# Attention outputs with tokens on partitions, row sums from a column of ones, and zero stores in portions

## The chip, the cores and the metric

The kernel runs on one core of a Trainium2 chip. Its time is the time on the device in microseconds (us). The engines are TensorE (PE, with its weight loads as PEld), VectorE (DVE), ScalarE (ACT), GpSimd (POOL) and SyncE (SP), which here only issues DMAs. Three timed runs of the kernel before and one profiled execution are at hand.

## The reference

Three stages follow each other: attention with a local window and some global columns, a dense MLP with the mish activation, and a mixture of eight experts with one expert per token.

```python
# q, k, v: [2, 8, 768, 64]; n_global = 8, n_local = 96
scores = q @ k.T / 8 - slope[h] * dist
keep = (col < n_global) | ((0 <= row - col) & (row - col < n_local))
a = exp(scores - max) where keep;  a = a / (sum(a) + 1e-9)
x = (a @ v) as [1536 tokens, 512]
h = x @ w_in;  x = (h * tanh(softplus(h))) @ w_out      # d_ff = 2048
e = argmax(x @ w_gate);  out = p[e] * (relu(x @ w1[e]) @ w2[e])   # 8 experts, d_ff = 1024
```

## The kernel before, in words

The 1536 tokens are cut into twelve tiles `t` of 128. A tile sees at most 232 columns of scores: 96 older tokens and 8 global ones (the part `c = 0`), and its own 128 (`c = 1`). Attention works in half tiles `s` (four of the eight heads each, 24 in all), through these steps:

- `a_S` (L285) makes the scores of four heads in PSUM, with queries on partitions.
- `a_max` (L295, DVE) adds the bias and takes the row maximum, `a_exp` (L312, ACT) the exponential. Its `accum_out` also writes the sum of the row into `rcs`, by an extra accumulator read on ACT.
- `a_T` transposes the probabilities on PE, and `a_Tev` (L354, ACT) copies them to `PT`, first part 0 and then part 1.
- `a_V` (L364) multiplies with the values. The values are the weights (64 columns, one head), `PT` is streamed (128 columns), and the output has channels on partitions and tokens along the free dimension, two heads in the two halves of the partitions.
- Because tokens lie along the free dimension there, the reciprocal row sums must be turned as well: `a_recip` (L319, DVE) adds 1e-9, inverts and spreads them to 512 columns, `a_R` transposes them on PE in four pieces, `a_Rc` (L333, ACT) copies them out of PSUM.
- `a_xm` (L387, DVE) multiplies outputs and reciprocals, `a_xh` (L396, ACT) rounds to float32r and `a_xl` (L400, DVE) forms the rest. Two tiles make a block of x, which is also stored for later passes.

The MLP works in 48 units `u` (three passes over w_in/w_out, six blocks of x): `L1_mms` (24 matmuls into `hp`), a chain of eleven mish steps on ACT and DVE that ends in `gh` and `gl`, and two units later `L2_mms` (12 matmuls into `acc`). The first ten units are interleaved with attention, two half tiles per unit. The MLP weights come as 32 chunks (`next_raw`), each converted in three parts by `next_conv`: part 0 is three integer operations on DVE, part 1 a rounding on ACT, part 2 a subtraction on DVE.

At the start an order written out by hand holds for all engines but SyncE, up to half tile 4. PE is kept busy by `fill` (a float32 matmul of the identity) while the first loads are under way. The two integers come by DMA and are needed for the bias (`bias_part`), the bias for the first `a_max`. From half tile 5 on the framework's scheduler sets the order of each engine by priority and its own prices, and may move independent work (such as conversions) forward. All loads are issued from SyncE, in its order; the integers from ACT. `load_v` brings 136 rows for a batch's first tile and 232 for the others. PSUM is one pool of eight banks.

Before the experts begin, the rows of their buffers `xg` are filled with zeros by `prefill`, 24 stores of 112 rows. It is called after unit 16:

```python
        if u == 16:
            prefill()
```

Of the kernel before, what the change touches and what calls it, by code (L numbers as in the profile page):

```python
# [34 lines left out]
NWARM = 17  # L35
# [7 lines left out]
def moe_kernel(ctx, tc, q, k, v, n_global, n_local, w_in, w_out, w_gate, w1, w2, out, dbg=None):  # L43
# [17 lines left out]
    int_raw = const.tile([128, 2, 2], I32, name="int_raw")  # L61
    for i_, src_ in enumerate((n_local, n_global)):
        nc.scalar.dma_start(int_raw[:, i_, :], src_.bitcast(I32).unsqueeze(0).broadcast_to([128, 2]))
# [4 lines left out]
    def make_ints():  # L68
        f = const.tile([128, 2, 2], F32, name="int_f")
        nc.vector.tensor_copy(f, int_raw)  # L70
        neg = const.tile([128, 2], F32, name="int_n")
        nc.vector.tensor_single_scalar(neg, f[:, :, 0], 0.0, op=ALU.is_lt)
        nc.vector.tensor_add(neg, neg, f[:, :, 1])
        nc.vector.scalar_tensor_tensor(out=nlg, in0=neg, scalar=4294967296.0, in1=f[:, :, 0],
                                       op0=ALU.mult, op1=ALU.add)

# [159 lines left out]
    def load_v(t):  # L236
        b, i = divmod(t, TPB)
        s0 = i * 128
        vv = at.tile([128, 2, DM], F32, tag="vv", name="vv")

        def ld(r0, n, col, tok):
            nc.sync.dma_start(vv[r0:r0 + n, col], v[b * S + tok:b * S + tok + n, :])

        if i == 0:
            ld(0, 128, 1, 0)
            nc.gpsimd.memset(vv[0:KR, 0], 0.0)
            ld(0, NG, 0, 0)
        elif i % 2 == 0:
# [3 lines left out]
        else:  # L252
# [29 lines left out]
    rcs = {}  # L282
    rbs = {}
# [11 lines left out]
    def a_max(s, q_):  # L295
        t, pr = divmod(s, 2)
        _, w, d0, _ = geom(t)
        if q_ == 0:
            Ps[s] = at.tile([128, 4, WN], F32, tag="P", name="P")
            mxs[s] = sm.tile([128, 4], F32, tag="mx", name="mx")  # L300
            if pr == 0:
                rcs[t] = sm.tile([128, H], F32, tag="su", name="su")
# [9 lines left out]
    def a_exp(s, q_):  # L312
        t, pr = divmod(s, 2)
        w = geom(t)[1]
        h = 4 * pr + q_
        nc.scalar.activation(out=Ps[s][:, q_, 0:w], in_=Ps[s][:, q_, 0:w], func=AF.Exp,  # L316
                             bias=mxs[s][:, q_:q_ + 1], scale=-1.0, accum_out=rcs[t][:, h:h + 1])

    def a_recip(t):  # L319
        su = rcs.pop(t)  # L320
        nc.vector.tensor_scalar_add(su, su, 1e-9)
        nc.vector.reciprocal(su, su)
        sp_ = xe.tile([128, ROW], F32, tag="x2", name="sp_")[:, 0:DM]
        nc.vector.tensor_copy(sp_.rearrange("p (a b) -> p a b", b=64), su.unsqueeze(2).to_broadcast([128, H, 64]))
        rbs[t] = sp_

    def a_R(t):
        rb = ps.tile([128, 4, 128], F32, tag="b", name="rb")
        for p_ in range(4):
            nc.tensor.transpose(rb[:, p_, :], rbs[t][:, p_ * 128:p_ * 128 + 128], ident)  # L330
        rbs[t] = rb

    def a_Rc(t):  # L333
        rs = xe.tile([128, ROW], F32, tag="x2", name="rs")[:, 0:DM].rearrange("p (a b) -> p a b", a=4)
        nc.scalar.copy(rs, rbs[t])
        rbs[t] = rs
# [27 lines left out]
    def a_V(s):  # L364
# [4 lines left out]
        if pr == 0:  # L369
            av_ps[t] = ps.tile([128, 4, 128], F32, tag="b", name="av")  # L370
        av = av_ps[t]
        va = vv[0:nk, 0]
        vb = vv[:, 1]
        for i in range(2):
            for c in range(2):
                for j in range(2):
                    q_ = 2 * i + j
                    h = 4 * pr + q_
                    hs = slice(h * 64, h * 64 + 64)
                    lh = va[:, hs] if c == 0 else vb[:, hs]  # L380
                    rh = PT[0:nk, 0, q_, :] if c == 0 else PT[:, 1, q_, :]
                    nc.tensor.matmul(av[64 * j:64 * j + 64, 2 * pr + i, :], lhsT=lh, rhs=rh,
                                     start=(c == 0), stop=(c == 1))
# [3 lines left out]
    def a_xm(t):  # L387
# [4 lines left out]
        xm = rbs.pop(t)  # L392
        nc.vector.tensor_mul(xm, av_ps.pop(t), xm)
        return xm

    def a_xh(t, xm):  # L396
        blk, o = divmod(t, 2)
# [1043 lines left out]
```

## Time and profile before

| what | value |
|---|---|
| three timed runs | 600.24, 602.90, 603.83 us, median 602.90 |
| profiled execution, its time | 601.62 us |
| its span | 599.8 us |
| busy: PE, DVE, ACT, POOL | 575.7 (96%), 480.0 (80%), 378.7 (63%), 88.4 us (15%) |
| DMA | 109.97 MB in 54935 packets |

The span is the time from the first to the last instruction of the profiled execution; its own time is 1.8 us longer. Busy shares are averages over stages that differ: attention with the first ten units lies before 157 us, the rest of the MLP up to about 385 us, the experts after it. Matmuls are pipelined, so a busy PE isn't PE at its peak.

### The profile page before, as it was taken

Reading aid. Unit: us, or ns where it says so; the run is one execution under the profiler, and the core shown is the slowest. Engines: PE = TensorE matmul, PEld = TensorE weight load, DVE = VectorE, ACT = ScalarE, POOL = GpSimd, SP = SyncE. Lnnn points to the kernel's source line nnn. Section 1 sums busy time; section 2 is a strip of 40 time slices with the busy share of each in tenths; the row PEclk is TensorE's granted clock in tenths of the full one; section 3 lists DMA queues with packets and bytes.
Section 4 is the critical chain, followed back from the end, with each engine's and each line's share of the span. In section 5 each row is a group of like instructions: output and inputs, shape, how many; then the busy total and the mean of one; then the engine's idle time right before and its main releaser. Section 6 shows DMA issues by size and latency. Waiting matters only on the chain.

```text
span 599.8 us, 11918 instructions
## 1 busy us (share of the span) xinstructions
PE 575.7 (96%) x4288; PEld 518.5 (86%) x4288; DVE 480.0 (80%) x1151; ACT 378.7 (63%) x882; POOL 88.4 (15%) x157
## 2 busy tenths in 40 slices
PE   8988999999999999999999999989999999999994
PEld 7766777777889899898989889779999999999994
DVE  5999999999699899776867667655985678888942
ACT  3898788898676565656455555465664566776731
POOL 3211210000110010010210301121201212113111
PEclk9999999999999999999999999999999999999998
DMA  7976555756899856322221310367667284586200
GB/s 225 343 246 190 179 209 172 241 191 229 282 304 300 326 187 227 113 71 80 98 89 54 106 36 36 114 251 281 203 243 251 96 310 164 199 307 235 106 18 22
DMA packets 54935, 109.97 MB, mean 183 GB/s; under 512 B 5723, under 2 KB 12891, under 8 KB 54866
## 3 DMA queue, kind: packets, MB, share of 16 engines
q1 hardware_dynamic: 48882, 90.21, 45.0%
q0 software_dynamic: 5696, 18.89, 9.6%
q8 instruction: 36, 0.59, 0.4%
q14 instruction: 33, 0.27, 0.1%
q10 hardware_dynamic: 288, 0.00, 0.0%
HBM read 84.67 MB, written 25.10 MB: 183 GB/s over the span
## 4 chain that ended last, share of the span: by engine, by line
PE 66%; DVE 15%; ACT 11%; DMA 5%; issue 2%; SPq 0%; POOL 0%; DVEq 0%; ACTq 0%; POOLq 0%
PE hp L441 18%; PE acc L460 16%; PE bacc L724 6%; PE bhp L724 6%; ACT P L316 3%; PE bacc L725 3%; PE bhp L725 3%; DVE P L305 2%; ACT PT L362 2%; DVE bw L158 2%; PE bhp L727 1%; PE bacc L727 1%; PE bacc L729 1%; PE bacc L728 1%; PE bhp L728 1%
## 5 line engine op out<-in xcount | busy, mean ns | idle before, releaser
L460 PE MATMUL acc<-wpair,gh 128*128 128x512 f32 x384 | 123.8, 400 | 1.4 <-ACT gh L497 1.4
L441 PE MATMUL hp<-xh,wpair 128*128 128x256 f32 x768 | 121.0, 287 | 2.3 <-ACT xh L398 2.2
L441 PEld LDWEIGHTS hp<-xh,wpair 128*128 128x128 f32 x768 | 104.3, 188 | 9.8 <-ACT xh L398 4.2
L460 PEld LDWEIGHTS acc<-wpair,gh 128*128 128x128 f32 x384 | 68.1, 188 | 16.5 <-issue 1.9
L158 DVE TENSOR_TENSOR bw<-bst,bw 128x512 fp32r<-128x512 f32 x112 | 72.9, 685 | 9.7 <-ACT bw L157 8.9
L157 ACT CAST bw<-bst 128x512 fp32r<-128x512 f32 x112 | 64.5, 620 | 19.6 <-PE bhp L728 9.8
L460 PE MATMUL acc<-wpair,gl 128*128 128x512 f32 x192 | 75.4, 393 | 0.8 <-DVE gl L500 0.8
L468 ACT ACTIVATE e<-hp 128x512 f32<-128x512 f32 x48 | 28.7, 598 | 71.3 <-PE hp L441 71.3
L441 PE MATMUL hp<-xl,wpair 128*128 128x256 f32 x384 | 63.9, 284 | 0.3 <-DVE xl L404 0.3
L724 PE MATMUL bhp<-xc,bw 128*128 128x352 f32 (+4 forms) x192 | 59.3, 364 | 0.7 <-DVE t L759 0.6
L724 PE MATMUL bacc<-hc,bw 128*128 128x352 f32 (+4 forms) x192 | 59.2, 364 | 0.0
L316 ACT ACTIVATE P<-P,mx 128x232 f32<-128x232 f32 (+1 forms) x96 | 44.7, 470 | 15.1 <-DVE mx L305 15.0
L441 PEld LDWEIGHTS hp<-xl,wpair 128*128 128x128 f32 x384 | 52.8, 188 | 1.0 <-DVE xl L404 0.9
L725 PE MATMUL bhp<-xc,bw 128*128 128x176 f32 (+4 forms) x192 | 48.5, 253 | 0.0
L725 PE MATMUL bacc<-hc,bw 128*128 128x176 f32 (+4 forms) x192 | 48.3, 252 | 0.0
L478 DVE SCALAR_TENSOR_TENSOR n<-n,r 128x512 f32<-128x512 f32 x48 | 33.1, 689 | 16.7 <-ACT r L476 15.9
L460 PEld LDWEIGHTS acc<-wpair,gl 128*128 128x128 f32 x192 | 36.1, 188 | 8.8 <-DVE gl L500 1.3
L500 DVE SCALAR_TENSOR_TENSOR gl<-n,gh 128x512 fp32r<-128x512 f32 x48 | 33.0, 688 | 11.6 <-ACT gh L497 10.6
L497 ACT ACTIVATE gh<-n 128x512 fp32r<-128x512 f32 x48 | 30.1, 628 | 13.4 <-DVE n L493 13.2
L472 ACT ACTIVATE n<-e 128x512 f32<-128x512 f32 x48 | 30.3, 632 | 13.1 <-DVE e L470 13.0
L724 PEld LDWEIGHTS bhp<-xc,bw 128*128 128x128 f32 x192 | 36.1, 188 | 1.7 <-DVE t L759 0.8
L423 POOL DMA_DIRECT2D xl<-xs x12 | 6.9, 576 | 204.9 <-PE hp L441 137.1
(220 smaller groups left out, 1278.2 us busy)
## 6 DMA issues: line engine op xcount, KB each, us to landing
bst<-in_moe_w_dram SPq DMA_DIRECT2D x56, 512.0 KB
wst<-in_moe_w_in_dram SPq DMA_DIRECT2D x16, 512.0 KB
wst<-in_moe_w_out_dram SPq DMA_DIRECT2D x16, 512.0 KB
xl<-xs POOLq DMA_DIRECT2D x12, 512.0 KB, 4.0
xh<-xs POOLq DMA_DIRECT2D x12, 512.0 KB, 4.9
xpl<-xps SPq DMA_DIRECT2D x24, 256.0 KB
xg<-z SPq DMA_DIRECT2D x24, 224.9 KB
w0f<-in_moe_w_dram SPq DMA_DIRECT2D x8, 512.0 KB
```

The costliest lines, as they stand in the source:

```text
L157: nc.scalar.copy(hi, src)
L158: nc.vector.tensor_sub(lo, src, hi.bitcast(F32))
L316: nc.scalar.activation(out=Ps[s][:, q_, 0:w], in_=Ps[s][:, q_, 0:w], func=AF.Exp, bias=mxs[s][:, q_:q_ + 1], scale=-1.0, accum_out=rcs[t][ ...
L441: yield lambda f=f, kk=kk, wi=wi, xx=xx, cs=cs: nc.tensor.matmul(hp[:, f, :], lhsT=w[:, wi, kk, cs], rhs=xx[:, kk, :], start=(kk == 0 and ...
L460: yield lambda f=f, o=o, cs=cs, gi=gi, wi=wi, first=first, last=last: nc.tensor.matmul(accs[b][o], lhsT=gi[:, cs], rhs=w[:, wi, f, :], sta ...
L468: nc.scalar.activation(out=e, in_=hp, func=AF.Exp, scale=-1.0)
L472: nc.scalar.activation(out=n, in_=e, func=AF.Square)
L478: nc.vector.scalar_tensor_tensor(out=n, in0=n, scalar=0.25, in1=r, op0=ALU.add, op1=ALU.mult)
L497: nc.scalar.mul(gts[u][0], n, -(2.0 ** -80))
L500: nc.vector.scalar_tensor_tensor(out=gl, in0=n, scalar=-(2.0 ** -80), in1=gh.bitcast(F32), op0=ALU.mult, op1=ALU.subtract)
L724: nc.tensor.matmul(o[:, 0:2 * cap], lhsT=wh, rhs=xc, start=first, stop=False)
L725: nc.tensor.matmul(o[:, 0:cap], lhsT=wl, rhs=xh, start=False, stop=last)
```

## The change

The roles in `a_V` are exchanged. `PT` is now the weight (64 tokens at a time) and the values are streamed: 64 columns of a head and a 65th that holds ones. The output has tokens on partitions, and its 65th column is the sum of the row. So `a_exp` writes no sum, and `a_recip`, `a_R` and `a_Rc` fall away. A new step `a_n` per half tile adds 1e-9 to the four sums, inverts them and multiplies the four heads, out of PSUM. Then `a_X` transposes the tile's 512 channels in four pieces, and `a_xh` and `a_xl` read its result in PSUM. Part 1 is now multiplied before part 0.

The tile of values has 65 columns per head; the ones are set by GpSimd, and the load writes 64 columns of each head, with a gap. The integers are loaded to one partition, and a matmul with a matrix of ones spreads them. There are 6 warm-up calls in place of 17, 3 calls after the integers, and the 4 later ones are gone. The order at the start is written anew around these steps; the loop is left to the scheduler as before. `prefill` becomes a generator, and three of its stores are made after each of the units 14 to 21.

```diff
-NWARM = 17
+NWARM = 6
...
-    int_raw = const.tile([128, 2, 2], I32, name="int_raw")
+    int_raw = const.tile([1, 2, 2], I32, name="int_raw")
...
-        nc.scalar.dma_start(int_raw[:, i_, :], src_.bitcast(I32).unsqueeze(0).broadcast_to([128, 2]))
+        nc.scalar.dma_start(int_raw[:, i_, :], src_.bitcast(I32).unsqueeze(0))
...
-    def make_ints():
-        f = const.tile([128, 2, 2], F32, name="int_f")
+    def make_ints(z, one, warm):
+        f = const.tile([1, 2, 2], F32, name="int_f")
...
-        neg = const.tile([128, 2], F32, name="int_n")
+        neg = const.tile([1, 2], F32, name="int_n")
...
-        nc.vector.scalar_tensor_tensor(out=nlg, in0=neg, scalar=4294967296.0, in1=f[:, :, 0],
+        nc.vector.scalar_tensor_tensor(out=z[0:1, :], in0=neg, scalar=4294967296.0, in1=f[:, :, 0],
...
+        nc.tensor.matmul(warm[:, 0:2], lhsT=one, rhs=z, start=True, stop=True)
+        nc.vector.tensor_copy(nlg, warm[:, 0:2])
...
     def load_v(t):
...
-        vv = at.tile([128, 2, DM], F32, tag="vv", name="vv")
+        vv = at.tile([128, 2, H, D + 1], F32, tag="vv", name="vv")
...
         def ld(r0, n, col, tok):
-            nc.sync.dma_start(vv[r0:r0 + n, col], v[b * S + tok:b * S + tok + n, :])
+            nc.sync.dma_start(vv[r0:r0 + n, col, :, 0:D],
+                              v[b * S + tok:b * S + tok + n, :].rearrange("p (h d) -> p h d", d=D))
+        def one(r0, n, col):
+            nc.gpsimd.memset(vv[r0:r0 + n, col, :, D:D + 1], 1.0)
+        one(0, 128, 1)
...
+            one(0, NG, 0)
...
-        elif i % 2 == 0:
+        else:
+            one(0, NPRE, 0)
+        if i > 0 and i % 2 == 0:
...
-        else:
+        elif i > 0:
...
-    rcs = {}
-    rbs = {}
+    xns = {}
+    xps_ = {}
...
     def a_S(s):
...
-            if pr == 0:
-                rcs[t] = sm.tile([128, H], F32, tag="su", name="su")
...
     def a_exp(s, q_):
...
-        h = 4 * pr + q_
...
-                             bias=mxs[s][:, q_:q_ + 1], scale=-1.0, accum_out=rcs[t][:, h:h + 1])
-    def a_recip(t):
...
-    def a_R(t):
...
-    def a_Rc(t):
...
+                             bias=mxs[s][:, q_:q_ + 1], scale=-1.0)
...
-        if pr == 0:
-            av_ps[t] = ps.tile([128, 4, 128], F32, tag="b", name="av")
-        av = av_ps[t]
-        va = vv[0:nk, 0]
-        vb = vv[:, 1]
-        for i in range(2):
-            for c in range(2):
+        av = ps.tile([128, 4, D + 1], F32, tag="b", name="av")
+        av_ps[s] = av
+        for q_ in range(4):
+            h = 4 * pr + q_
+            for c in (1, 0):
+                n = nk if c == 0 else 128
...
-                    q_ = 2 * i + j
-                    h = 4 * pr + q_
-                    hs = slice(h * 64, h * 64 + 64)
-                    lh = va[:, hs] if c == 0 else vb[:, hs]
-                    rh = PT[0:nk, 0, q_, :] if c == 0 else PT[:, 1, q_, :]
-                    nc.tensor.matmul(av[64 * j:64 * j + 64, 2 * pr + i, :], lhsT=lh, rhs=rh,
-                                     start=(c == 0), stop=(c == 1))
+                    r = slice(64 * j, 64 * j + 64)
+                    nc.tensor.matmul(av[r, q_, :], lhsT=PT[0:n, c, q_, r], rhs=vv[0:n, c, h, :],
+                                     start=(c == 1), stop=(c == 0))
...
-    def a_xm(t):
+    def a_n(s):
+        t, pr = divmod(s, 2)
+        av = av_ps.pop(s)
+        if pr == 0:
+            xns[t] = xe.tile([128, ROW], F32, tag="x2", name="xn")[:, 0:DM]
+        su = sm.tile([128, 4], F32, tag="su", name="su")
+        nc.vector.tensor_scalar_add(su, av[:, :, D], 1e-9)
+        nc.vector.reciprocal(su, su)
+        nc.vector.tensor_tensor(out=xns[t][:, 256 * pr:256 * pr + 256].rearrange("p (a b) -> p a b", b=D),
+                                in0=av[:, :, 0:D], in1=su.unsqueeze(2).to_broadcast([128, 4, D]), op=ALU.mult)
+    def a_X(t):
+        xn = xns.pop(t)
+        xp = ps.tile([128, 4, 128], F32, tag="b", name="xp")
+        for p_ in range(4):
+            nc.tensor.transpose(xp[:, p_, :], xn[:, p_ * 128:p_ * 128 + 128], ident)
+        xps_[t] = xp
+    def a_xh(t):
...
-        xm = rbs.pop(t)
-        nc.vector.tensor_mul(xm, av_ps.pop(t), xm)
-        return xm
-    def a_xh(t, xm):
-        blk, o = divmod(t, 2)
-        nc.scalar.copy(xT[blk][0][:, :, o * 128:o * 128 + 128], xm)
-    def a_xl(t, xm):
+        nc.scalar.copy(xT[blk][0][:, :, o * 128:o * 128 + 128], xps_[t])
+    def a_xl(t):
...
-        ins = nc.vector.tensor_sub(xl[:, :, cs], xm, xh[:, :, cs].bitcast(F32)).ins
+        ins = nc.vector.tensor_sub(xl[:, :, cs], xps_.pop(t), xh[:, :, cs].bitcast(F32)).ins
...
-    def a_x(t):
-        xm = a_xm(t)
-        a_xh(t, xm)
-        return a_xl(t, xm)
...
     def x_reload(blk):
...
-    pass
+                yield
+    zero_rows = prefill()
...
+        wi = ps.tile([128, 512], F32, tag="b", name="wi")
+        one = tmp0.tile([128, 128], F32, name="one")
+        z = tmp0.tile([128, 2], F32, name="z")
+        nc.vector.memset(one, 1.0)
+        nc.vector.memset(z, 0.0)
...
-        make_ints()
+        make_ints(z, one, wi)
+        fill(3)
...
-        some(b0, 4)
+        some(b0, 3)
...
-        some(b0, 5)
+        some(b0, 6)
...
-        fill(4)
...
-        a_recip(0)
...
-        a_S(3)
-        heads(a_exp, 2)
...
+        a_S(3)
+        heads(a_exp, 2)
         heads(a_max, 3)
...
+        a_n(0)
+        a_V(1)
...
-        a_R(0)
...
+        a_Tev(2, 0)
+        a_Tev(2, 1)
+        a_n(1)
+        load_v(2)
...
-        a_V(1)
-        load_v(2)
+        a_X(0)
...
-        a_Tev(2, 0)
-        a_Tev(2, 1)
-        a_recip(1)
-        a_Rc(0)
...
-        next_conv(0)
...
+        a_xh(0)
+        next_conv(1)
...
-        a_R(1)
+        a_n(2)
+        next_conv(0)
...
         load_v(3)
+        a_n(3)
+        next_conv(1)
         a_S(4)
-        a_Rc(1)
-        next_conv(1)
-        x0 = a_xm(0)
-        a_xh(0, x0)
-        x1 = a_xm(1)
-        a_xh(1, x1)
-        next_conv(1)
-        a_xl(0, x0)
-        xlast = a_xl(1, x1)
+        a_X(1)
+        a_xh(1)
+        a_xl(0)
+        xlast = a_xl(1)
...
-            if s % 2 == 0 and s > NS:
-                a_recip(s // 2 - 1)
...
-            if s % 2 == 0:
-                a_R(s // 2 - 1)
-                a_Rc(s // 2 - 1)
...
+            a_n(s - 1)
...
-                a_x(s // 2 - 1)
+                a_X(s // 2 - 1)
+                a_xh(s // 2 - 1)
+                a_xl(s // 2 - 1)
...
-        if u == 16:
-            prefill()
+        if 14 <= u < 22:
+            for _ in range(CAPMAX // 112):
+                next(zero_rows, None)
...
```

## Rows read from the trace of the kernel before

**Rows 1.** Table by stretches: start, length, engines' busy us (instructions), clock, DMA share, GB/s.

```profile
10.80:25.50 14.70, 14.24 (x144) 11.06 (x142) 13.39 (x56) 13.87 (x46) 4.17 (x11) 1.00 1.06 333
25.50:145.40 119.90, 112.62 (x915) 89.06 (x913) 117.14 (x338) 100.86 (x275) 10.55 (x13) 1.00 0.64 211
...
157.00:199.60 42.60, 42.60 (x277) 39.00 (x278) 38.97 (x72) 27.75 (x48) 3.57 (x7) 1.00 1.07 321
```

**Rows 2.** Waits of DVE and PE from 25.5 to 145.4: us, times, longest.

```profile
DVE n L478 <- ACT r L476: 0.9, 2, 0.4
...
PE av L382 <- ACT PT L362: 1.9, 6, 0.5
PE hp L441 <- ACT xh L398: 1.7, 2, 1.4
```

**Rows 3.** Chain of waits up to 27 us: start, us, what.

```profile
1.29 5.36 DMA int_raw<-in_n_global_dram
...
10.81 0.30 DVE P L305
...
12.88 0.30 PE pt L347
...
22.14 0.60 PE rb L330 x4
...
24.60 0.63 ACT xh L398
```

**Rows 4.** Table by stretches, the first loads; columns as in rows 1.

```profile
4.00:6.30 2.30, 2.30 (x12) 2.30 (x12) 0.00 (x0) 0.00 (x0) 0.66 (x4) 1.00 0.55 136
6.30:9.30 3.00, 2.34 (x17) 2.18 (x16) 2.38 (x11) 0.00 (x0) 0.54 (x1) 1.00 1.11 374
```

**Rows 5.** DMA issues of the whole span: count, median us to landing.

```profile
out_dram<-yo,idi POOLq DMA_INDIRECT x19, 3.1
```

**Rows 6.** Timeline of PE, four places: start, us, line, operation, count.

```profile
1.67 6.89 PE L863 MATMUL warm<-ident 128*128 128x128 f32 x34 [1.67 <-POOL ident masks.py:199]
...
10.35 1.16 PE L863 MATMUL warm<-ident 128*128 128x128 f32 x8
...
18.99 1.10 PE L382 MATMUL av<-PT,vv 72*64 72x128 f32 x16
...
277.56 1.11 PE L555 MATMUL lp<-wg,xt 128*64 128x8 f32 x32
```

**Rows 7.** Instruction groups of DVE, 25.5 to 145.4: count, busy us, mean ns, idle.

```profile
L172 DVE SCALAR_TENSOR_TENSOR cv<-wst,cv 128x512 int32<-128x512 int32 x20 | 14.3, 714 | 0.1
...
L393 DVE TENSOR_TENSOR rs<-av,rs 128x512 f32<-128x512 f32 x9 | 6.2, 684 | 0.2
...
L321 DVE TENSOR_SCALAR su<-su 128x8 f32<-128x8 f32 x9 | 2.3, 254 | 0.0
...
L322 DVE RECIPROCAL su<-su 128x8 f32<-128x8 f32 x9 | 1.7, 194 | 0.0
...
L324 DVE COPY sp__1526<-su 128x512 f32<-128x512 f32 x1 | 0.4, 422 | 0.0
```

**Rows 8.** Instruction groups of ACT, 25.5 to 145.4; columns as in rows 7.

```profile
L316 ACT ACTIVATION_READ_ACCUMULATOR P<-P,mx 128x1 f32 x76 | 14.6, 192 | 0.0
...
L335 ACT COPY rs<-rb 128x512 f32<-128x512 f32 x9 | 5.1, 568 | 0.0
```

**Rows 9.** DMA queues, 6.4 to 7.0 and 8.3 to 9.5: packets, MB, share.

```profile
q1 hardware_dynamic: 414, 0.21, 114.8%
...
q1 hardware_dynamic: 243, 0.46, 105.0%
```

**Rows 10.** Timeline of SyncE's issues from 155, and of PE at 200.9.

```profile
158.76 6.91 SPq L618 DMA_DIRECT2D xg<-z  x9
...
184.88 0.43 SPq L182 DMA_DIRECT2D wst<-in_moe_w_in_dram  x1
...
200.90 0.50 PE L460 MATMUL acc<-wpair,gl 128*128 128x512 f32 x1 [0.83 <-DVE gl L500]
```

More of the change, by code (lines that the diff above doesn't have):

```diff
@@ L314, in a_exp @@
         w = geom(t)[1]
-        h = 4 * pr + q_
         nc.scalar.activation(out=Ps[s][:, q_, 0:w], in_=Ps[s][:, q_, 0:w], func=AF.Exp,
-                             bias=mxs[s][:, q_:q_ + 1], scale=-1.0, accum_out=rcs[t][:, h:h + 1])
-    def a_recip(t):
[L320 to L325, printed above, removed]
-    def a_R(t):
[L328 to L331, printed above, removed]
-    def a_Rc(t):
-        rs = xe.tile([128, ROW], F32, tag="x2", name="rs")[:, 0:DM].rearrange("p (a b) -> p a b", a=4)
-        nc.scalar.copy(rs, rbs[t])
-        rbs[t] = rs
+                             bias=mxs[s][:, q_:q_ + 1], scale=-1.0)
     pts = {}
```

## The prediction

> **What bounds the kernel now.** I read the table by stretches first. From 25.5 to 145.4 us, the attention loop, VectorE (DVE) is busy 117.1 of 119.9 us, TensorE (PE) 112.6, ScalarE (ACT) 100.9 and the DMA engines 64% [rows 1]. The list of waits then tells which of the two full engines leads: DVE's longest wait there is 0.9 us in all, PE's 1.9 us and more beside it [rows 2]. So DVE sets the pace, with PE 7 us behind, and work taken from ACT alone is worth little. After the loop PE is busy in every microsecond of 157.0 to 199.6, DVE in 39.0 of 42.6 [rows 1]: whatever ends the loop earlier ends the kernel earlier by as much. Last I read the chain of waits of the start. It begins with a DMA: the two integers, 5.36 us from issue to landing, and then goes through DVE to the first row maximum at 10.81; from 12.88 to 22.74 it stays on PE, and the first block of x is copied at 24.60 [rows 3].
>
> **The integers.** Now each is broadcast by the DMA to 128 partitions, and while these tiny transfers run the engines move 136 GB/s at 55% busy; right after, with the same q and k loads queued, 374 GB/s [rows 4]. After the change each integer is one 8-byte row. The trace has no such load; the nearest landing of a small transfer is 3.1 us [rows 5]. Bounds: nothing gained (5.36 us again), or 3.1 us, which is 2.26 less. I take the whole 2.26, because the queue beside it gets free too. Against it stand a matmul that broadcasts the value and a copy: estimated 0.6 us, three small DVE-like steps of about 0.2 [rows 7]. Net -1.65 us for the first maximum, between -3 (if q and k land earlier too, which the 374 GB/s would allow) and +0.6.
>
> **Warm-up.** 17 float32 calls (34 records) took 6.89 us, 203 ns each, and a later group of 8 records 1.16 us, 145 ns each [rows 6]: by that, most of the first group ran at the lower of the two clock levels, 1.2 GHz, and the upper (which the clock column shows for every stretch from 10.8 on [rows 1]) came only near its end. The change keeps 6 calls, then a pause for the integers, then 4 more. I expect the first scores at 1.2 GHz. PE holds the chain for 9.9 us, from 12.88 on [rows 3]. Bounds: 0, if the clock rises before that stretch, and +4 if some 8 us of it run at half speed. I take +0.5, since PE waits for ACT at its beginning anyway.
>
> **The output matmuls.** Now a half tile's `a_V` is 8 calls, 64 weight columns and 128 streamed, taking 1.10 us. It becomes 16 calls of 64 weight columns and 65 streamed. Streamed columns stay the same (1024 against 1040), weight loads double. The row that prices this is that of the gate's logits: 32 records of the same 64 weight columns with 8 streamed, alternating between the two column halves in the same way, in 1.11 us [rows 6]. There only the loads can count, so 32 of them cost 1.1 us, and if the 65 columns are streamed behind them the new `a_V` costs 1.1 us as well: nothing. The four transposes for the reciprocals go, the four of `a_X` come: nothing, but they now stand after the outputs.
>
> The Trainium skill, "TensorE: Matmul & The Clock Gate", Part 3, section "The mechanism", says that a weight load overlaps running matmuls only where the row group differs. Here all row groups are the same. By that rule the old row would need more than the 1.10 us that it shows: the trace disagrees, and the cost by the rule is the third rival below.
>
> **VectorE and ScalarE.** Per tile DVE loses an addition, a reciprocal, the spreading copy and the product with the outputs: 0.25 + 0.19 + 0.42 + 0.68 = 1.55 us [rows 7]. It gains two times an addition, a reciprocal and a product over 256 elements read from PSUM. The last has no row; bounds are half and all of the 512-wide product, 0.34 and 0.68; I take 0.42, a fixed part of 0.16 and half of the rest. With additions at 0.17 to 0.25 that is 1.56 to 1.74. So DVE gains 0.1 us a tile, +1 us in the loop's ten tiles (bounds -1.5 and +7). ACT loses 8 accumulator reads of 192 ns and a copy of 0.57 us a tile [rows 8], 2.1 us, some 20 us in the loop, but DVE waits for ACT about 1 us there [rows 2]; with the startup's end I allow -1.5. What hides the rest is DVE's own queue. Loop together: -0.5.
>
> **Values in pieces.** The loads of v leave a gap after every 64 elements, so a 2 KB row goes as eight packets of 256 B. 414 packets of 512 B took 114.8% of 16 engines in 0.6 us, 26.6 ns each; 243, nearly all of 2 KB, 105% in 1.2 us, 83 ns each [rows 9]. A 256 B packet then costs between 13.3 (half) and 26.6 ns; on the line through both points 17. A row costs +55 ns (bounds +23 and +130). There are 2 x 136 + 10 x 232 = 2592 rows: +8.9 us of the engines (3.7 to 21), over a loop where they are 64% busy: hidden. At the start, tiles 0 and 1 (368 rows) add 1.3 us where the engines are full [rows 1]; behind them in SyncE's queue stand k, q and the weight chunks. None of these is on the chain now [rows 3], so I book nothing; if the cover goes, it is 1.3 us (0.5 to 3). GpSimd gets two small fills per tile. It is busy 10.6 of 119.9 us [rows 1], but a v load may have to wait for its fill, and the loads behind it on SyncE with it; v is fetched a tile ahead, so I count zero.
>
> The Trainium skill, "DMA: Bandwidth & Descriptors", section "Specifications", puts the smallest transfer at full rate at 512 B, with read-modify-write below. No row here shows a 256 B packet. By the rule the price lies at the upper end, 21 us of engine time, still inside the loop's idle third.
>
> **Zero stores.** Now 24 stores stand close together on SyncE (nine of them in a row from 158.76), and a weight chunk is first issued again at 184.88. The chunks behind it are late, and PE stands 0.83 us for `gl` at 200.90 [rows 10]. Three stores per unit should let the chunk through: -0.8 (bounds -0.83 and +1, because the stores now run beside the reloads of x).
>
> **The sum.** -1.65 + 0.5 - 0.5 - 0.8, and for the startup's end, where a copy of the reciprocals and a product give way to `a_n`, `a_X` and the copy, -0.5: -2.95 us. The profiled execution took 601.62 us (span 599.8), the three others 600.24, 602.90 and 603.83; their mean of 602.15 less 2.95 gives 599.2. I forecast 599 with a range of its own of 596 to 603.
>
> **Rivals.**
> - The loop gives more. Twenty weight conversions are done on DVE inside it, the third of four operations alone 14.3 us [rows 7], about 2.5 us each by three like it and a shorter one. Nothing in the loop needs most of them yet; the scheduler puts them where it thinks DVE free. With ACT lighter it may leave two or three to the time after, where DVE has 3.6 us free in 42.6 [rows 1]: -5 to -7.5, so 592 (588 to 596). Against it: the order comes from the scheduler's own prices, which no row shows. Chance 0.24.
> - The earlier start is eaten: PE stays at 1.2 GHz through the dense part, or the 256 B packets hold the first chunks. -1.65 becomes +1: 602. Chance 0.12.
> - Slower: the doubled weight loads are not hidden behind streaming, so that each pair is loaded and then streamed. Then a half tile costs the loads, 1.1, plus 16 pairs of 65 columns at 0.07 us (half of 1.10 / 8), 1.1 more: 20 half tiles in the loop make +22 us. It decides once it exceeds PE's 7 us behind DVE: +15, so 614. For it: the doubling is certain. Against it: both rows of 1.1 us [rows 6]. Chance 0.08.
> - x comes later. `a_n`, `a_X` and the copy now follow the last outputs, where before the transposes were done ahead. PE already waits 1.7 us for xh [rows 2]; 1.3 us more for each of five blocks makes +6.5: 606. Chance 0.06.
>
> **How the numbers follow.** The forecast keeps 0.50. A measurement of this kernel tells about 1%, 6 us, from no change. Below 596.9 lie nearly all of the first rival (0.22) and the low edge of the forecast (0.10): 0.32. Above 608.9 lie the third rival and the upper end of the fourth: 0.10. Between: 0.58. The range of 591 to 607 leaves out some 0.09 below and 0.10 above.
>
> **What would show it.** The integers' DMA no longer heads the chain, and the first maximum comes near 9.2 us. New `a_V` groups of 32 records take about 1.1 us (2.2 says the third rival). DVE stays above 95% in the loop with 20 conversions (17 or 18 say the first). No wait of PE near 200. If the loop's length changes by more than 3 us either way, the step that fails is that DVE's work is the same.

## The result, and the profile after

The changed kernel takes 609.38 us (median of four), the kernel before 601.91 beside it: ratio 1.0125, 95% interval 1.0078 to 1.0172. It is slower by 7.5 us, where 599.0 was forecast and 591 to 607 allowed. The profiled execution took 611.5 us, the slowest of the four; its span is 609.8.

The table by stretches first, with the columns of [rows 1]. The first line is the kernel before again, now up to unit 10, so that the loop is taken whole, with its tail: from the first matmul of unit 0 to that of unit 10. So "loop" is meant from here on.

```profile
25.40:156.90 131.50, 123.63 (x1002) 97.97 (x1000) 124.80 (x357) 109.52 (x296) 12.90 (x19) 1.00 0.64 211
```

The kernel after: the loop, and before it the startup in three parts.

```profile
26.50:166.00 139.50, 126.69 (x1321) 102.44 (x1321) 125.42 (x380) 99.55 (x206) 15.05 (x35) 0.99 0.67 210
...
3.00:15.50 12.50, 9.62 (x94) 7.82 (x95) 7.64 (x48) 6.04 (x16) 2.58 (x9) 1.00 1.06 264
15.50:18.90 3.40, 3.40 (x42) 2.71 (x39) 2.45 (x14) 1.63 (x4) 2.13 (x4) 0.50 0.99 351
18.90:26.50 7.60, 6.94 (x102) 5.34 (x100) 5.75 (x15) 4.36 (x8) 1.15 (x7) 1.00 0.92 213
```

Unit 0 begins 1.1 us later (26.5 against 25.4), and the loop is 8.0 us longer (139.5 against 131.5). DVE's work in the loop is the same (125.4 against 124.8). What grew is the time in which DVE stands: 6.7 us before, 14.1 now. PE's grew from 7.9 to 12.8. Unit 10, the first behind the loop, takes 7.1 us against 5.8, with the granted clock at 0.50 from 165.7 to 169.1. From then on a unit takes 5.65 us in both kernels, and the wait at 200 us [rows 10], which took 1.1, is gone. With 0.7 us more in the experts, 1.1 + 8.0 + 1.4 - 1.1 + 0.7 is about the 10.0 us between the two profiled spans; the medians are 7.5 apart.

The 8.0 us aren't spread evenly. Units 1, 2 and 9 take 2.8, 2.4 and 1.8 us more than before, the other seven 0.9 together. Unit 2 holds 3.4 us at a granted clock of 0.50 (56.5 to 59.9); the kernel before has no such stretch in its loop.

Waits of PE in the loop (us, times, longest), the kernel before:

```profile
PE av L382 <- ACT PT L362: 1.9, 6, 0.5
PE hp L441 <- ACT xh L398: 1.7, 2, 1.4
PE rb L330 <- DVE sp__566 L324: 1.1, 1, 1.1
```

and after, with the one wait of ACT that the kernel before doesn't have:

```profile
PE av L365 <- ACT PT L350: 5.0, 6, 2.4
PE xp L385 <- DVE xn L378: 4.0, 3, 1.4
PE hp L431 <- ACT xh L393: 2.3, 4, 0.7
...
ACT xh L393 <- PE xp L385: 11.0, 8, 2.2
```

PE waits for the scaled outputs (`xn`), and 3.1 us more for the probabilities' copies (`PT`). Ahead of the longest wait for `PT`, 2.42 us, mish steps and an exponential stand in front of the copies on ACT:

```profile
47.95 0.72 ACT L464 ACTIVATE r<-n,cqs 128x512 f32<-128x512 f32 x1
48.58 0.61 ACT L487 ACTIVATE gh<-n 128x512 fp32r<-128x512 f32 x1
...
49.10 0.47 ACT L323 ACTIVATE P<-P,mx 128x232 f32<-128x232 f32 x1
49.47 1.05 ACT L350 COPY PT<-pt 104x512 f32<-104x512 f32 x2
...
50.58 0.63 PE L365 MATMUL av<-vv,PT 128*64 128x65 f32 x14 [2.42 <-ACT PT L350]
```

That ACT's own waits for `xp`, further ahead, push these copies back is not shown. How the chain from the outputs to x looks, at the loop's end, in the timeline of the kernel after (start, us, engine, line, operation, idle time before it):

```profile
161.04 1.16 PE L365 MATMUL av<-vv,PT 128*64 128x65 f32 x32 [0.45 <-ACT PT L350]
...
162.31 0.69 DVE L468 SCALAR_TENSOR_TENSOR n<-n,r 128x512 f32<-128x512 f32 x1 [2.94 <-ACT r L466]
...
162.91 0.15 DVE L376 TENSOR_SCALAR su<-av 128x4 f32<-128x4 f32 x1
...
163.03 0.69 DVE L470 SCALAR_TENSOR_TENSOR r<-n,r 128x512 f32<-128x512 f32 x1
...
163.64 0.17 DVE L377 RECIPROCAL su<-su 128x4 f32<-128x4 f32 x1
...
163.76 0.69 DVE L472 TENSOR_TENSOR e<-e,r 128x512 f32<-128x512 f32 x1
...
164.37 0.42 DVE L378 TENSOR_TENSOR xn<-av,su 128x256 f32<-128x256 f32 x1
...
164.84 0.44 PE L385 MATMUL xp<-ident,xn 128*128 128x128 f32 x2 [1.29 <-DVE xn L378]
165.31 0.59 ACT L393 CAST xh<-xp 128x512 fp32r<-128x512 f32 x1 [1.14 <-PE xp L385]
...
165.95 0.58 PE L431 MATMUL hp<-xh,wpair 128*128 128x256 f32 x1 [0.68 <-ACT xh L393]
```

From the last output (161.04 + 1.16) to the next unit's first matmul pass 3.75 us. The three small operations of `a_n` take 0.74 us, but a mish step stands ahead of each of them: DVE does them in its queue's order. In the kernel before the same stretch is 1.87 us, because transposes and copy of the reciprocals are done ahead of the outputs. The loop has five such places, one per block of x. Measured so on PE's timeline they sum to 17.7 us after and 11.3 before: 1.3 us more at each on average (0.9 to 1.9). Not all of this is waiting, since PE does other work there, now the transposes too: it stands 5.1 us of the 17.7 and 2.3 of the 11.3. In the middle of a block (ahead of units 3, 5, 7 and 9) the same stretch grew by 0.8 to 1.2 us, though PE doesn't stand there in either kernel.

### The profile page after: what moved, and what is told of

It reads as the page before. It is cut to its first block, busy times and chain, and to the rows that moved or that the text cites. A ratio compares the mean times of both kernels' runs of the same rounds, so it can differ in the third digit from the quotient of the medians.

```text
span 609.8 us, 12591 instructions
## 1 busy us (share of the span) xinstructions
PE 578.8 (95%) x4650; PEld 522.1 (86%) x4650; DVE 478.0 (78%) x1178; ACT 366.0 (60%) x774; POOL 88.8 (15%) x181
## 4 chain that ended last, share of the span: by engine, by line
PE 76%; DVE 10%; ACT 5%; DMA 5%; issue 2%; SPq 1%; POOL 0%; DVEq 0%; POOLq 0%; ACTq 0%
PE hp L431 22%; PE acc L450 19%; PE bhp L715 4%; PE bacc L715 4%; PE av L365 3%; PE sp L302 2%; DMA bst<-in_moe_w_dram 2%; PE bhp L716 2%; PE bacc L716 2%; DVE bw L160 2%; PE bhp L734 2%; PE bhp L718 1%; PE bacc L718 1%; PE bacc L720 1%; PE bacc L719 1%
## 5 line engine op out<-in xcount | busy, mean ns | idle before, releaser
L431 PE MATMUL hp<-xl,wpair 128*128 128x256 f32 x384 | 65.9, 288 | 0.0
L323 ACT ACTIVATE P<-P,mx 128x232 f32<-128x232 f32 (+1 forms) x96 | 40.5, 471 | 16.6 <-DVE mx L313 16.6
L365 PEld LDWEIGHTS av<-vv,PT 128*64 128x64 f32 (+2 forms) x768 | 25.4, 141 | 14.2 <-ACT PT L350 8.9
L715 PEld LDWEIGHTS bhp<-xc,bw 128*128 128x128 f32 x192 | 36.1, 188 | 1.6 <-DVE t L750 0.7
L716 PEld LDWEIGHTS bhp<-xc,bw 128*128 128x128 f32 x192 | 36.7, 191 | 0.0
L716 PEld LDWEIGHTS bacc<-hc,bw 128*128 128x128 f32 x192 | 36.7, 191 | 0.0
```

The costliest lines, as they stand in the source:

```text
L365: nc.tensor.matmul(av[r, q_, :], lhsT=PT[0:n, c, q_, r], rhs=vv[0:n, c, h, :], start=(c == 1), stop=(c == 0))
L431: yield lambda f=f, kk=kk, wi=wi, xx=xx, cs=cs: nc.tensor.matmul(hp[:, f, :], lhsT=w[:, wi, kk, cs], rhs=xx[:, kk, :], start=(kk == 0 and ...
L715: nc.tensor.matmul(o[:, 0:2 * cap], lhsT=wh, rhs=xc, start=first, stop=False)
L716: nc.tensor.matmul(o[:, 0:cap], lhsT=wl, rhs=xh, start=False, stop=last)
```

## Experiments

Theory A: the values' 256 B pieces are late, at the start above all. Theory B: x comes later in each block; B1 because the scheduler lets other work go first, B2 because links of DVE's chain always have something between them. Theory C: the new start throws the loop out of step. All ratios are to the kernel before, run beside each. "Late x" is the sum over the five places just described, "at 0.50" the time in the loop (us) with the granted clock at the lower level. The last four columns come from one profiled execution of each kernel; that of the changed kernel was the slowest of its four, that of run 11 the fastest of its nine.

| run | ratio [95%] | median us | unit 0 at | loop | late x | at 0.50 |
|---|---|---|---|---|---|---|
| before | 1 | 601.9 to 603.4 | 25.4 | 131.5 | 11.3 | 0 |
| changed kernel | 1.0125 [1.0078, 1.0172] | 609.4 | 26.5 | 139.5 | 17.7 | 3.7 |
| 1 wide rows | 1.0091 [1.0053, 1.0128] | 608.0 | 26.0 | 138.0 | 17.0 | 6.8 |
| 2 pieces only | 0.9999 [0.9968, 1.0031] | 602.9 | 25.4 | 132.0 | 11.6 | 3.4 |
| 3 zero stores only | 0.9961 [0.9932, 0.9990] | 600.6 | 25.0 | 132.0 | 11.6 | 3.4 |
| 4 integers only | 1.0003 [0.9969, 1.0037] | 602.5 | 23.2 | 131.6 | 11.2 | 0 |
| 5 new start, old loop | 1.0033 [1.0005, 1.0062] | 604.5 | 25.6 | 133.2 | 12.7 | 6.8 |
| 6 old start, new loop | 1.0117 [1.0078, 1.0156] | 610.4 | 25.6 | 136.7 | 16.9 | 0 |
| 7 priority | 1.0117 [1.0085, 1.0149] | 610.9 | 25.6 | 141.9 | 16.8 | 10.2 |
| 8 no addition | 1.0013 [0.9985, 1.0040] | 603.6 | 25.3 | 133.7 | 15.7 | 0 |
| 9 addition beside | 1.0069 [1.0038, 1.0100] | 605.6 | 25.2 | 137.1 | 16.0 | 3.4 |
| 10 part 0 first | 1.0105 [1.0077, 1.0134] | 608.1 | 26.5 | 136.5 | 17.6 | 0 |
| 11 old outputs, rest new | 0.9937 [0.9918, 0.9957] | 598.7 | 23.0 | 130.3 | 11.4 | 0 |
| 12 new loop, no addition | 1.0005 [0.9977, 1.0032] | 603.2 | 24.5 | 135.2 | 15.7 | 0 |
| 13 old outputs, late reciprocals | 1.0017 [0.9997, 1.0036] | 603.7 | 23.3 | 135.5 | 17.9 | 3.4 |
| 14 pinned, no addition | 1.0141 [1.0107, 1.0175] | 610.1 | 24.1 | 132.8 | 13.2 | 3.4 |
| 15 pinned, addition | 1.0138 [1.0112, 1.0165] | 610.5 | 24.3 | 129.9 | 13.4 | 0 |
| 16 run 11, no addition | 0.9926 [0.9904, 0.9948] | 597.2 | 23.4 | 130.2 | 11.9 | 3.4 |
| 17 mish pinned, addition | 1.0020 [0.9992, 1.0048] | 603.9 | 22.9 | 134.1 | 14.8 | 0 |
| 18 mish pinned, no addition | 1.0062 [1.0034, 1.0091] | 606.8 | 23.0 | 137.1 | 15.0 | 10.2 |

**Runs 1 and 2: the pieces.** Run 1 takes them out of the changed kernel, run 2 puts them into the kernel before.

```diff
# 1 (values with their ones laid out in DRAM, no GpSimd fills)
-nc.sync.dma_start(vv[r0:r0 + n, col, :, 0:D], ...rearrange("p (h d) -> p h d", d=D))
+nc.sync.dma_start(vv[r0:r0 + n, col], ...rearrange("p (h d) -> p h d", d=D + 1))
# 2
-nc.sync.dma_start(vv[r0:r0 + n, col], v[...])
+nc.sync.dma_start(vv[r0:r0 + n, col, :, 0:D], v[...].rearrange("p (h d) -> p h d", d=D))
```

> The changed kernel, but the values lie in DRAM with a 1 after every 64 elements, so that a row comes as one piece of 2,080 B and GpSimd sets no ones. Theory A (the 256 B pieces make the values of the first tile late, PE stands 1.6 us for them, its clock falls to the lower level and the startup loses some 4 us; later loads are late too): the first unit begins near 22.5 us in place of 26.5, units 1 to 3 lose their extra 5 us, and the time is 600 to 604. Theory B (x comes later in every block, whatever the pieces cost): the wait for the first values goes, but the loop stays some 8 us longer than before, and the time is 605 to 608, at most 4 us under the changed kernel.

> The kernel before, with the values loaded in 256 B pieces into the tile of 65 columns per head, and nothing else: the engines' orders stay. Theory A: the start suffers as it does in the changed kernel, and the time rises by 3 to 8 us, to 605 to 610. Theory B: the pieces are hidden behind the other loads, and the time stays within 1.5 us of the kernel before.

Run 2 settles it: the pieces alone change nothing beyond 0.3% either way. Run 1 keeps nearly all of the loss; its loop is within 1.5 us of the changed kernel's. Theory A falls as an account of the loss, even for the start: there PE waits 1.45 us for the first values with whole rows too, against 1.61 with pieces.

**Runs 3 and 4: two parts alone.** In the kernel before, `prefill` as a generator with three stores after each of the units 14 to 21; and `int_raw` on one partition with the matmul that spreads it, `NWARM = 6` and `fill(3)`, the four later calls kept.

> The kernel before, with the zero stores in portions of three after units 14 to 21 and nothing else. Both theories: -0.8 to -1.2 us (the wait at 200 us goes, which took 1.1 us out of the unit). A rival (stores beside the reloads of x delay something else): 0 to +1.

> The kernel before, with the integers on one partition and spread by a matmul, 6 warm-up calls and 3 after the integers (the 4 later calls stay) and nothing else. If the early start is worth what it looked like: first maximum near 7.6 us and not 10.8, first unit at 22.5 to 23 and the time -2.5 to -3. If the clock is lost with the warm-up calls (a stretch at the lower level, as in the changed kernel): the first unit near 25, and the time -1 to +1.

The stores give 0.4%, 2.4 us, with an interval that holds the 0.8 to 1.2. The integers bring unit 0 forward by 2.2 us in the profile, without a stretch at the lower clock. The timed runs don't show it: the interval ends at a gain of 1.9 us, short of the 2.5 expected. Run 11 has both.

**Runs 5 and 6: start and loop apart.** Tiles 0 and 1 in one way, tiles from 2 on in the other.

```diff
# 5, on the changed kernel: for tiles t >= 2
+acc = dict(accum_out=rcs[t][:, h:h + 1]) if t >= 2 else {}
+a_recip(s // 2 - 1); a_R(s // 2 - 1); a_Rc(s // 2 - 1)
-a_V(s - 1); a_n(s - 1); a_X(s // 2 - 1); a_xh(s // 2 - 1); a_xl(s // 2 - 1)
+a_V_o(s - 1); a_x(s // 2 - 1)      # the functions of the kernel before
# 6, on the kernel before: the reverse for t >= 2
```

> The changed kernel's start (tiles 0 and 1 in the new way, integers, warm-up, spread zero stores, values in pieces), but from tile 2 on outputs and reciprocals as in the kernel before. Theory B (the loss sits in the loop, because x comes later there): the first ten units take as long as before, and only the start's loss of about 1 us stays against the zero stores' gain of 1 to 2: 600 to 603. Theory C (the new start throws the loop out of step, or its late values do): units 1 and 2 stay long, and the time is 605 or more.

> The other half: the start of the kernel before (tiles 0 and 1, integers, warm-up) and its zero stores, and from tile 2 on the new outputs. Theory B: the loop is some 7 us longer than before, 608 to 611. Theory C: 602 to 604.

The larger loss goes with the new outputs in the loop: 1.17%, on the old start and the old integers, and a loop 5.2 us longer without any time at the lower clock. Not all of run 6's loss lies there, though. In its profile the last dense unit begins 4.3 us later than before, and 5.0 more are lost in the experts, whose code the edit leaves as it is (3.6 there in run 5, -1.4 to +1.5 in all others). No run explains these. The new start isn't free either. Run 5 has the gaining parts of run 11 and its loop, and is 5.8 us slower (604.5 against 598.7): unit 0 comes 2.6 us later, and the loop takes 2.9 more (4.1 in units 1 and 2, of which the other units give back 1.2). In run 5's loop 6.8 us lie at 0.50, in run 11's none, so a part of the 2.9 is the clock. So theory B carries most, theory C a part. How the start loses is seen in the changed kernel, in the timelines of PE and DVE:

```profile
11.95 0.34 PE L365 MATMUL av<-vv,PT 128*64 128x65 f32 x4
13.89 1.04 PE L365 MATMUL av<-vv,PT 72*64 72x65 f32 x28 [1.61 <-DMA vv<-in_v_dram]
14.86 1.32 PE L302 MATMUL sp<-kT,qr 64*128 64x232 f32 x8
```
```profile
7.59 0.30 DVE L313 CUSTOM_DVE_ANT_0 P<-sp,ndist 128x136 f32<-128x136 f32 x1 [0.15 <-PE sp L302]
...
16.32 0.40 DVE L313 CUSTOM_DVE_ANT_0 P<-sp,ndist 128x232 f32<-128x232 f32 x1 [3.63 <-PE sp L302]
```

The first maximum is at 7.59 (10.81 before, [rows 3]). But the new order puts the outputs of half tile 0 ahead of the scores of half tile 3. Their values have not landed, PE stands 1.61 us, the scores come late and DVE stands 3.63 us. From 1.6 us behind the end of PE's stand, the granted clock is 0.50 for 3.4 us (second startup line of the table of stretches above). Run 1 has nearly the same stand and no such stretch, and its unit 0 begins 0.5 us earlier.

**Runs 7 and 8: which link.** Run 7 traces `a_n`, `a_X`, `a_xh` and `a_xl` inside `tc.high_priority()`. Run 8 drops the addition:

```diff
-nc.vector.tensor_scalar_add(su, av[:, :, D], 1e-9)
-nc.vector.reciprocal(su, su)
+nc.vector.reciprocal(su, av[:, :, D])
```

> The changed kernel, with the scaling of the outputs, the transposes, the rounding and the subtraction traced at high priority in the loop, so that the scheduler takes them as soon as it thinks them ready. Theory B1 (x is late because the scheduler lets other work go first): the tail's 3.85 us from the last output to the first matmul of the next unit shrink toward 2.5, and the time falls by 2 to 6 us under the changed kernel, 603 to 607. Theory B2 (x is late because the scheduler always puts one other operation between two small dependent ones, whatever the priority): within 1.5 us of the changed kernel.

> The changed kernel, without the addition of 1e-9 (the reciprocal reads the sum in PSUM; the sum is at least 1). One link of DVE's chain goes, and with it the operation that stands between it and the next. Theory B2: 1 us per block at the block's end, -3 to -5 us against the changed kernel, 604 to 606. If DVE's work alone counts (24 additions of 0.16): at most -2, so 607 or more.

Priority doesn't change the time, so B1 falls: at the loop's end the same three mish steps still stood ahead of the links. One operation on four elements less gives 1.1%. That is more than was expected, and more than its 20 x 0.158 us of work. In run 8's loop ACT's wait for `xp` falls from 11.0 to 4.1 us and PE's for `xn` from 4.0 to 0.6:

```profile
ACT xh L392 <- PE xp L384: 4.1, 7, 1.1
...
PE xp L384 <- DVE xn L377: 0.6, 1, 0.6
```

PE's waits for `PT` stay, at 4.6 us: they don't follow ACT's wait for `xp`. A part of the 6.7 us goes with the clock. Run 8 has no stretch at 0.50 in the loop or in unit 10, the changed kernel 6.8 us in the two; over the timed runs the granted clock is 0.996 in the median, against 0.9915.

**Runs 9 and 10.** Run 9 keeps the addition, into a tile that nobody reads, behind the product. Run 10 has `for c in (0, 1)` for `(1, 0)` in `a_V`.

> The changed kernel with the addition of 1e-9 kept as work but taken out of the chain: the reciprocal reads the sum in PSUM, the product follows, and the addition is made beside them into a tile that nobody reads. Theory B2 (what counts is the length of the chain from outputs to x): product 1.4 us after the outputs, as without the addition, and 603 to 606. If DVE's work counts (20 x 0.17 us = 3.4 in the loop): 607 to 609.

> The changed kernel with part 0 of the probabilities multiplied before part 1 in each head, as in the kernel before, so that the first outputs need only the first of ACT's two copies. If PE's waits for the copies lengthen the loop (0.57 us a copy, 20 half tiles): -2 to -5, so 604 to 607. If they come from the order on ACT, where both copies stand behind the mish steps: within 1.5 of the changed kernel.

Run 9 lies between the two: by the ratios 0.56% above run 8 and 0.56% under the changed kernel. Taken as they stand, about half of what the addition costs is its link in the chain, half its work in DVE's queue. The intervals of neighbours overlap or nearly touch, so the halves are rough. Run 10 stays within 1.5 us of the changed kernel, its second forecast, so the order of the two parts isn't it.

**Runs 11 and 12: the gaining parts together.** Run 11 is runs 3 and 4 in one. Run 12 adds to it the new outputs from tile 2 on, without the addition.

> The kernel before with the two parts of the change that gained when done alone: the spread zero stores, and the integers on one partition with fewer warm-up calls. Outputs, values and order stay as before. If the parts add up: first unit near 23, no wait at 200, and -2.5 to -3.5 us: 599 to 600. If the earlier start is lost in units 1 and 2: -1 to -2.

> Old start with the early integers, spread zero stores, and from tile 2 on the new outputs without the addition. Theory B2: first unit near 23, loop near 134 as without the addition, 600 to 602. If the new outputs have something else against them beside the chain: 604 or more.

Run 11 beats both kernels: 0.9937, 3.8 us under the kernel before. Against it the new outputs cost 4.5 us even in their shorter form, with 0.9 us less work on DVE (122.66 against 123.59 in the loop, in their tables by stretches). Late x is 4.3 us larger. Run 12's 603.2 us lies between its two forecasts, and its unit 0 begins 1.5 us later than run 11's.

**Run 13: the same chain with the old outputs.** The transposes of the reciprocals are queued on PE behind the tile's last output. Not one operation is added.

```diff
+vlast = a_V(s - 1)
+pe(2)
 if s % 2 == 0:
-    a_R(s // 2 - 1)
+    with tc.issue_after(vlast):
+        a_R(s // 2 - 1)
     a_Rc(s // 2 - 1)
-a_V(s - 1)
-pe(2)
```

> The old outputs (kernel of run 11), but the four transposes of the reciprocals are queued on PE behind the tile's last outputs, so that transposes, ACT's copy, the product and the rounding follow each other behind them, with not one operation more. Theory B (x comes later): the loop grows by 4 to 8 us and the time is 603 to 607. If the rest of the new outputs' loss comes from something else (weight loads, PSUM tiles): within 1.5 us of run 11, 598 to 600.

It costs 5.0 us against run 11 (603.7 against 598.7; 0.8% by the ratios, whose intervals are apart), and the loop 5.2. PE's waits in the loop of run 11:

```profile
PE hp L443 <- ACT xh L400: 2.3, 3, 1.6
PE av L384 <- ACT PT L364: 2.0, 6, 0.5
```

and of run 13:

```profile
PE hp L444 <- ACT xh L401: 6.5, 5, 2.0
PE av L384 <- ACT PT L364: 3.3, 8, 0.7
```

4.2 us more for `xh` and 1.3 for `PT`, together 5.5: a loss like that of the new outputs (4.5 in run 12), made without them. In all, PE stands 11.4 us in this loop and 6.6 in run 11's; that alone is nearly the 5.2. Run 13's loop also has 3.4 us at 0.50, run 11's none. Weight loads and PSUM tiles are not needed to explain it. Theory B stands.

**Runs 14 and 15: nothing between the links.** On run 12, the mish steps and conversions that follow are queued behind the product; run 15 has the addition again.

```diff
-chain(u - 1, 7, 8)  /  chain(u, 2, 3); next_conv(0)
+with tc.issue_after(mul):
+    chain(u - 1, 7, 8)  /  chain(u, 2, 3); next_conv(0)
```

> The kernel of run 12 (new outputs without the addition, old start), with the mish steps and conversions that are traced after the product pinned behind it on DVE, so that reciprocal and product stand together. Theory B2: product under 1 us after the outputs in place of 1.46, and 1 to 3 us faster than run 12: 600 to 602. If the interleaved operations don't matter: 603 (pinning may also cost something, up to 605).

> The same with the addition of 1e-9 back in the chain. Theory B2: with nothing between, the addition costs its own 0.17 us per half tile, at most 3.5 us: 602 to 605, clearly under the changed kernel's 608 to 609. If pinning doesn't help: 607 or more.

Both miss in time, and tell most. Run 15's loop, then two stretches behind it (table by stretches), and its conversions in the loop (instruction groups: count, busy us, mean ns):

```profile
24.30:154.20 129.90, 121.50 (x1321) 100.65 (x1321) 104.66 (x346) 95.93 (x199) 14.50 (x35) 1.00 0.59 182
...
154.20:199.70 45.50, 45.50 (x300) 41.72 (x301) 45.22 (x83) 29.19 (x50) 4.24 (x8) 1.00 0.93 297
199.70:245.00 45.30, 39.02 (x231) 33.97 (x230) 45.30 (x84) 25.98 (x43) 3.17 (x6) 0.96 0.98 307
```
```profile
L210 DVE TENSOR_TENSOR wpair<-cv,wpair 128x512 fp32r<-128x512 f32 x13 | 8.8, 684 | 0.4 <-ACT wpair L208 0.3
```

With the addition in the chain, but nothing between its links, the new outputs have the shortest loop of all, 129.9 us. Seven of the 20 conversions were pushed behind it, where DVE is full (45.22 of 45.5, then 45.30 of 45.30) and PE stands 6.3 us, of which 5.9 for the mish results `gh`, as here:

```profile
218.49 0.73 PE L531 MATMUL acc<-wpair,gh 128*128 128x512 f32 x2 [2.92 <-ACT gh L568]
```

Mish steps and conversions alternate on DVE there, so what the loop gave was lost behind it. DVE has 20 us less work in this loop than in that of the kernel before, and the loop is only 1.6 us shorter; PE is busy in 121.5 of its 129.9 us, so 8.4 is the most that could have come off. Run 14, without the addition, is no faster than run 15, and its loop is longer.

**Run 16: the addition of the old way.** Run 11 without `tensor_scalar_add` in `a_recip`.

> The kernel of run 11 without the addition of 1e-9 (one per tile, 0.25 us on DVE). Were the loop bound by DVE's work: -2.5 us (10 x 0.25), 596. If reciprocals are off the path and DVE's idle time takes it up: within 1 us of run 11.

0.1% under run 11 by the ratios (1.5 us by the medians), with intervals that overlap; the loop is the same, though with 3.4 us at 0.50. Against 6.7 us that the smaller addition is worth in the new chain: the old one stands ahead of the outputs, off the path.

**Runs 17 and 18: mish steps pinned, conversions free.** `next_conv(0)` leaves the `with` of runs 14 and 15.

> As run 15 (new outputs with the addition, old start), but only the mish steps are pinned behind the product; conversions are free, and about as many as in the kernel before stand in the loop. If the chain alone lengthens the loop: loop 130 to 134 and 598 to 602. If VectorE's conversions between its links matter as much: loop 135 to 138 and 603 to 607.

> The same without the addition. If the chain alone counts: 598 to 601. If the conversions between the links matter: 1.5 to 4 us under run 17, since one link and one conversion per half tile leave the chain.

All 20 conversions are back in the loop. Its length with the addition goes from 139.5 us to 136.7 with the old start (run 6), to 134.1 with the mish steps pinned (run 17, which has the early integers too) and to 129.9 with the conversions pinned as well (run 15). That fits an account by which both kinds of work between the links count, but the last step also takes 19 us of DVE's work out of the loop (123.4 to 104.7), so the two aren't told apart. Run 17 itself lies between its forecasts: the loop meets the first, the time of 603.9 the second.

Run 18 is a miss: less work, but 3 us more. PE stands as long in its loop as in run 17's (9.7 and 9.6 us). What is longer is PE's busy time, 127.3 against 124.5, and 10.2 us of that loop lie at 0.50, none of run 17's. The timed runs agree, with a granted clock of 0.9885 in the median against 0.9945. So the difference goes with the lower clock; what brought that on was not tried.

## Why the prediction was wrong

**The step that failed** is the first: "So DVE sets the pace", and with it "Loop together: -0.5". DVE's work was foreseen rightly (+0.6 us over the loop's ten units; +1 forecast), as were its 20 conversions; the loop still took 8.0 more, and DVE's share of it fell from 95% to 90%, where over 95% was forecast. The term that was put at nothing without a reason stands with the output matmuls: the transposes cost "nothing, but they now stand after the outputs". Where a product and a rounding followed the last outputs, an addition, a reciprocal, a product, transposes and a rounding follow now, on DVE, PE and ACT in turn, each working its queue in order. Run 13 shows what such a longer chain costs: 5.0 us, with not one operation more. DVE was full because the scheduler fills its gaps with conversions that nothing waits for at once. Take 20 us of DVE's work away, and the loop hardly gets shorter (run 15).

The text gave the sign that should have decided, a loop changed by over 3 us, but tied it to the wrong step: that "DVE's work is the same" held.

**The right rival had 0.06.** "x comes later" was priced at 1.3 us for each of five blocks, 6.5 in all, 606. Measured in these five places: 1.3 us on average, in a loop 8.0 us longer. The mechanism is right, and run 13 shows it alone; that the number fits is luck. Of the 6.4 us there PE stands only 2.8, and most of the loop's loss lies in units 1, 2 and 9. What the rival left out is that PE also waits 3.1 us more for the copies of the probabilities (why isn't shown), that the clock falls, and that the start loses too.

**The integers** gained more than said in the profiles: 3.2 us at the first maximum against 1.65, and 2.2 to 2.4 at unit 0 where the old order stays (runs 4 and 11); in the timed runs of run 4 nothing of it is seen. **"Startup's end -0.5"** failed: the new order gives 2.6 us back up to unit 0 and 2.9 in the loop (run 5 against 11). The rival "The earlier start is eaten" came true in size, with unit 0 at +1.1, but by neither of its causes. The first scores ran at the upper clock (3.00 to 15.50 in the table of stretches), so the +0.5 for the **warm-up** wasn't paid there (three calls follow the integers, not four), and runs 4 and 11, with as few calls ahead of the scores, have no stretch at the lower clock before the end. The pieces aren't it by run 1. What the trace shows is the new order, in which PE comes to the outputs before their values have landed.

**ACT's work** fell by 10.0 us in the loop (109.5 to 99.6), not by some 20: an accumulator read takes 192 ns, but the next operation begins 0.09 to 0.10 us after its start (61.80 and 61.89 in the kernel before), so the means can't be added up.

**The output matmuls** were right: 32 records take 1.16 us at the upper clock, 1.1 forecast, and the third rival is out. The Trainium skill's rule on weight loads that was set against the rows ("TensorE: Matmul & The Clock Gate", Part 3, "The mechanism") doesn't hold for this row either, as far as it goes by the row group: 32 loads and 32 streams of 65 columns, all in one row group, take 1.16 us together. **Values in pieces**: hidden, as said (run 2). **Zero stores**: -0.8 forecast, 1.1 in the unit that held the wait, 0.4% in the timed runs. **Conversions that leave the loop** were priced as a gain of 5 to 7.5 us in the first rival. When they did leave, PE stood 5.0 us (run 14) and 6.3 us (run 15) behind it for `gh` and `gl`.

What stays open: how the 6.7 us of the addition divide between its latency, its work, the lower clock and the order that the scheduler finds around it; why leaving it out gains nothing where the mish steps are pinned (run 14 against 15, run 18 against 17); why PE waits longer for the copies of the probabilities; and what runs 5 and 6 lose in the experts.

## What to carry to other kernels

A busy share near 100% bounds a stage only if that work can't wait; ask which of it is filler, what the stage would take without it, and what the filler would hold up elsewhere. When a rival's price comes out, look unit by unit whether the time lies where the rival put it. Count the links between a stage's last product and the first use of its result, with what stands ahead of each link in its engine's queue: reciprocals made before the outputs are free here, and made behind them they cost 5 us with not one operation more. Test the parts of a change one by one: two of this one gained 3.8 us together, the part that gave it its name lost more.

## What the runs showed of the hardware beside that

TensorE's granted clock fell to the lower of its two levels after PE had stood: to 0.50 from 15.5 to 18.9 us in the changed kernel, after 1.61 us of waiting for values, and in run 5 from 52.1 to 58.9, around 2.72 us of waiting for `xh`:

```profile
49.90:52.10 2.20, 0.39 (x4) 0.03 (x2) 2.11 (x9) 2.20 (x6) 2.20 (x4) 1.00 0.32 72
52.10:58.90 6.80, 5.89 (x30) 5.66 (x32) 6.21 (x15) 4.96 (x14) 0.52 (x1) 0.50 0.99 283
```

So a stand of PE can be paid for twice: unit 10 takes 7.1 us with 3.4 at 0.50, and 5.8 in the kernel before without. It isn't always: after 1.45 us of waiting at run 1's start no such stretch follows. Issuing loads also takes longer when they are cut in pieces: SyncE spent 6.38 us on four issues of values in the changed kernel, and 1.64 on three with whole rows (run 1); how much of it is waiting isn't shown.

```profile
5.58 6.38 SPq L244 DMA_DIRECT2D vv<-in_v_dram  x4
```
```profile
3.98 1.64 SPq L244 DMA_DIRECT2D vv<-in_v_dram  x3
```
